# Issue order of the first decay loads, and longer rows in the w_in loads, in a fused state-space and feed-forward kernel

## The chip, the core and the metric

The kernel runs on one core of a Trainium2 chip. The time is device time in microseconds (us) of one execution; the median of the runs of the kernel before is 116.85 us. A core has a matrix engine (TensorE, PE in the profile; PEld is its weight load), VectorE (DVE), ScalarE (ACT), GpSimd (POOL) and SyncE (SP). Each works through its own instructions in order. DMAs are issued here by SP and ACT (SPq and ACTq in the profile) and carried by 16 DMA engines.

## The reference

A chunked state-space scan, followed by a feed-forward layer with a tanh-approximated GELU. In short, for x of shape (4, 8, 768, 32), decays a of shape (4, 8, 768), B and C of shape (4, 8, 768, 16):

```python
cum = np.cumsum(np.log(np.clip(a, 1e-6, 1)), axis=-1)      # within a chunk
M = (C @ B.T) * causal * np.exp(cum[i] - cum[j])
y = M @ x + (C @ state) * np.exp(cum)
state = np.exp(sum) * state + (B * decay_from_j).T @ x
# then, on y as (3072 tokens, 256):
h = y @ w_in                       # w_in: (256, 2048)
out = gelu_tanh(h) @ w_out         # w_out: (2048, 256)
```

All inputs and the output are fp32; the kernel multiplies in bf16.

## The kernel before

The scan works on chunks of Q = 128 positions, six to a batch entry, 24 in all; two chunks make a unit u (12 units). For each unit the kernel forms G = B C^T for all heads (f_G), masks it (f_M, on VectorE), transposes nothing more but multiplies by x and by the carried state (f_Y), and copies the result to SBUF as bf16 (f_yev, into xm). The decays are folded into B and C beforehand: the decay products are made by a scan (f_Rq), turned (f_tpq), inverted (f_recip0) and multiplied into C (f_mulc) and B (f_mulb). Each unit then goes through the feed-forward layer: eight pieces of the first matrix (f_s1, line 709), eight GELUs on ScalarE (f_gelu, line 713), and eight pieces of the second (f_s2, line 727) whose sum is copied out (f_oev) and stored.

The order of all this is written out by hand in the string ORDERED: each word is a step, a letter behind the colon is the engine (A = ScalarE, D = VectorE, P = GpSimd, S = SP), and ~n emits n filler matmuls of 128 columns on a zero matrix (function fill, line 697), grouped into matmuls of up to 512 columns. A step's instructions are emitted at its place, and every engine executes its own in that order. So a step that waits holds all later steps of its engine.

At the start, four loads (load_aq.0 to load_aq.3, line 159) fill aq_t, the decays of the first four chunks, one 32-row part each; f_clipq on VectorE needs all four. load_bc0.1 and load_bc0.0 (line 150) load C and B of the first four chunks, load_x4 (line 183) x of the same chunks, load_a.0 and load_a.1 (line 162) the remaining decays. Then come the weights: load_wi.0 to load_wi.3 (line 190) bring w_in in four blocks of 512 columns, both halves k of its 256 rows in one load; load_wo.0 to load_wo.3 (line 194) bring w_out in four blocks. A weight block lands as fp32 in a tile wf; two casts turn it into bf16: wi.q.k casts columns q*512 to (q+1)*512 of half k, wo.q.k half of a block of w_out. In the order string wi.0.0, wi.0.1, wi.1.0 and wi.3.0 are on ScalarE, wi.1.1, wi.2.0, wi.2.1 and wi.3.1 on GpSimd, where wo.0.1 stands ahead of wi.2.1; wo.0.0 is on VectorE.

s1.u.i computes columns i*256 to (i+1)*256 of the hidden layer for unit u, four matmuls; so s1.0.0 and s1.0.1 need wi.0.0 and wi.0.1, s1.0.2 and s1.0.3 need wi.1.0 and wi.1.1, s1.0.4 and s1.0.5 need wi.2.0 and wi.2.1.

Other steps that are spoken of: peq and ppq (the decay of a whole chunk, spread by a matmul at line 356 and copied by pendq); tw.i (transposes of C and B for the first four chunks, line 425) and ew (their copies out of PSUM); XX (matmuls that bring x of the first four chunks into row order, line 563) and xn.c (their copies, on ScalarE); XD.u (products of B and x, line 573), which are written into the same PSUM tiles that xn reads; S.u.k and SP.c (state updates on VectorE, lines 676 and 683); pp and pend (decays of all chunks, lines 393 and 314); mul1, T1, tp2 (the decayed B and C of chunks 4 and 5).

Of the kernel before, what the change touches and what calls it, by code (L numbers as in the profile page):

```python
# [8 lines left out]
FP32 = mybir.dt.float32  # L9
# [7 lines left out]

SCR = (2, 3)
ORDERED = """
c_wz c_ident c_zero c_unp load_aq.2:A load_bc0.1 c_tri load_aq.1:S load_aq.3:S load_aq.0:A c_m8  # L20
c_sel c_warm c_m4 load_bc0.0 load_x4 clipq Rq tpq load_a.0:A load_a.1:S peq ~53 ppq pendq:A
load_wi.0 c_cz c_bmask recip0 mulc.0:D mulc.1:D mulb:P ~9 tw.1 tw.0 ew.0.0:D c_par ew.0.1:A tw.2
ew.0.2:A x4.1:D ~8 G.0 clip ew.1.0:A ew.1.1:A load_wi.1 M.0.0 GE.3 x4.0:P GE.2 load_wi.2 ~2 XX.0
# [64 lines left out]
def kernel(  # L88
# [10 lines left out]
    nc = tc.nc  # L99

    batch, H, S, D = x.shape
# [20 lines left out]
    wfp = ctx.enter_context(tc.tile_pool(name="wfp", bufs=WFB))  # L122
# [22 lines left out]
    XF, X16, WF = {}, {}, {}  # L145
# [39 lines left out]
    wi = moe_w_in.rearrange("(k d) f -> d k f", d=128)  # L185
    wo = moe_w_out.rearrange("(q p k) m -> q p k m", p=128, k=4)

    def load_wi(q):
        WF[("i", q)] = wfp.tile([128, 2, 512], FP32, name="wf")
        nc.sync.dma_start(out=WF[("i", q)], in_=wi[:, :, q * 512:(q + 1) * 512])  # L190

    def load_wo(q):
        WF[("o", q)] = wfp.tile([128, 4, d_model], FP32, name="wf")
# [100 lines left out]
    w_in_sb = const.tile([128, 2, d_ff], BF16, name="w_in_sb")  # L294
# [17 lines left out]
    def copy(eng, o, i):  # L312
        if eng == "ACT":
            nc.scalar.activation(o, i, AF.Copy)  # L314
        elif eng == "POOL":
            nc.gpsimd.tensor_copy(out=o, in_=i)  # L316
        else:
            nc.vector.tensor_copy(out=o, in_=i)  # L318

    def f_wi(q, k, eng):  # L320
        copy(eng, w_in_sb[:, k, q * 512:(q + 1) * 512], WF[("i", q)][:, k])

    def f_wo(q, k, eng):
        copy(eng, w_out_sb[:, 4 * q + 2 * k:4 * q + 2 * k + 2], WF[("o", q)][:, 2 * k:2 * k + 2])
# [418 lines left out]
    def add(eng, fn, *args, deps=(), alt=""):  # L743
        name = ".".join([fn.__name__.removeprefix("f_"), *map(str, args)])
        s = steps[name] = Step(name, eng, None, deps, alt or eng)
        if alt:
            s.fn = lambda: fn(*args, {"A": "ACT", "D": "DVE", "P": "POOL", "S": "SP"}[s.eng])
        elif fn is f_s1:
            s.fn = lambda: fn(*args, s.pre)
        else:  # L750
            s.fn = lambda: fn(*args)
        return s
# [6 lines left out]
    bl = {(b, i): add("S", load_bc, b, i) for b in range(1, batch) for i in (1, 0)}  # L759
    xl = {u: add("S", load_x, u) for u in range(2, NU)}  # L760
    wl = {(k, q): add("S", f, q) for k, f in (("i", load_wi), ("o", load_wo)) for q in range(4)}

    win = {(q, k): add("P", f_wi, q, k, alt="PAD", deps=[wl[("i", q)]]) for q in range(4) for k in range(2)}
    won = {(q, k): add("P", f_wo, q, k, alt="PAD", deps=[wl[("o", q)]]) for q in range(4) for k in range(2)}
    for q in range(4):
        wl[("i", q)].takes("wf", win[(q, 0)], win[(q, 1)])
        wl[("o", q)].takes("wf", won[(q, 0)], won[(q, 1)])

    ccz, cid, ctri, cbm, cm8 = (add("P", f) for f in (c_cz, c_ident, c_tri, c_bmask, c_m8))
# [130 lines left out]
    for u in range(NU):  # L900
        for i in range(NI):
            q = (2 * i + 1) // 4
# [21 lines left out]
    for w in ORDERED.split():  # L924
        if w[0] == "~":
            fill(yb, int(w[1:]))
        else:
            w, _, n = w.partition("+")
            name, _, e = w.partition(":")
# [33 lines left out]
```

## Time and profile before

| | |
|---|---|
| runs of the kernel | 116.79 and 116.91 us, median 116.85 |
| span of the profiled execution, first to last instruction | 115.1 us |
| what the median has around that span | 1.75 us |
| TensorE busy | 109.4 us (95%) |
| ScalarE, VectorE, GpSimd busy | 75.1, 68.7, 15.1 us |
| DMA | 15.97 MB, mean 139 GB/s; issues of SP from 0.80 us on |

The profile is of one execution. Its own time outside the span is not recorded; the difference of 1.75 us stands in the table as the difference of the median and the span.

How to read the lines: the time line gives start, duration, engine, line of the kernel, operation, out<-in and the shapes, xN for N instructions merged, and in brackets the idle time of the engine before them with what ended it. The view by windows gives for a stretch its length, then the busy time of each engine in it with the number of instructions, then the granted TensorE clock, the mean busy share of the DMA engines and GB/s. DMA landings give the size and the time from issue to landing in us. The chain of work that ended last gives start, duration and what ran.

### The profile page before, as it was taken

What the parts mean: (1) busy time and instruction counts of PE and PEld (TensorE: products, weight loads), DVE (VectorE), ACT (ScalarE), POOL (GpSimd) and SP (SyncE); (2) the same over time, 40 slices, a digit from 0 to 9 for tenths busy, and PEclk for the clock granted to TensorE, in tenths of its full rate; (3) what the DMA queues carried; (4) which work ended last, traced back from release to release, by engine and by line L of the source; (5) the groups of instructions that cost most, each with busy time, mean ns of one, the idle gap of its engine ahead of it and who ended that gap; (6) DMA issues with size and microseconds to landing.
All of it is one profiled execution on the core that took longest, in us unless ns stands there. A gap on an engine that the chain in (4) does not pass through costs nothing.

```text
span 115.1 us, 3372 instructions
## 1 busy us (share of the span) xinstructions
PE 109.4 (95%) x1425; PEld 92.2 (80%) x1425; DVE 68.7 (60%) x135; ACT 75.1 (65%) x149; POOL 15.1 (13%) x32
## 2 busy tenths in 40 slices
PE   6999799999999999999999999999999999999990
PEld 2354578978877979799898998998989989999970
DVE  6688799998799989196966281546827421000100
ACT  3119889978657767657576486377766765685710
POOL 6564274122220000020002000000000000000000
PEclk9999999999999999999999999999999999999999
DMA  2999999949969828959478760000014014001132
GB/s 65 236 280 286 397 293 311 278 84 218 225 109 226 214 64 203 192 147 265 102 158 184 174 178 0 6 0 0 0 50 138 0 49 139 0 0 51 46 103 79
DMA packets 43006, 15.97 MB, mean 139 GB/s; under 512 B 36656, under 2 KB 41456, under 8 KB 42992
## 3 DMA queue, kind: packets, MB, share of 16 engines
q1 hardware_dynamic: 42848, 15.68, 53.9%
q8 instruction: 11, 0.18, 0.6%
q10 hardware_dynamic: 144, 0.08, 0.4%
q14 instruction: 3, 0.02, 0.1%
HBM read 11.04 MB, written 3.93 MB: 130 GB/s over the span
## 4 chain that ended last, share of the span: by engine, by line
PE 82%; DMA 8%; SPq 4%; POOL 1%; issue 1%; ACT 0%
PE hp L709 36%; PE o_ps L727 33%; DMA wf<-in_moe_w_out_dram 8%; PE yb L727 3%; PE ga L595 3%; PE yb L650 2%; PE yb L659 2%; SPq L190 1%; PE hp L628 1%; SPq L162 1%; SPq L159 1%; SPq L150 1%; POOL w_out_sb L316 1%; POOL w_in_sb L316 1%; SPq L183 1%
## 5 line engine op out<-in xcount | busy, mean ns | idle before, releaser
L713 ACT ACTIVATE gT<-hp 128x512 bf16<-128x512 f32 x96 | 53.3, 595 | 24.5 <-PE hp L709 24.0
L709 PE MATMUL hp<-xm,w_in_sb 128*128 128x256 bf16 x384 | 51.9, 273 | 0.5 <-ACT pend L314 0.3
L727 PE MATMUL o_ps<-w_out_sb,gT 128*128 128x256 bf16 x352 | 46.4, 273 | 0.0
L709 PEld LDWEIGHTS <-w_in_sb 128*128 128x128 bf16 x384 | 41.2, 114 | 3.2 <-issue 1.7
L727 PEld LDWEIGHTS <-gT 128*128 128x128 bf16 x384 | 37.0, 98 | 4.7 <-issue 0.8
L318 DVE COPY o_sb<-o_ps 128x256 f32<-128x256 f32 x7 | 3.0, 424 | 22.4 <-PE o_ps L727 18.4
L605 DVE TENSOR_TENSOR m<-ga,tri 128x1024 bf16<-128x1024 f32 x12 | 14.6, 1216 | 0.0
L605 DVE TENSOR_TENSOR m<-gb,tri 128x1024 bf16<-128x1024 f32 x11 | 13.4, 1219 | 0.5 <-PE gb L595 0.5
L697 PE MATMUL yb<-wz 128*128 128x512 bf16 (+2 forms) x24 | 8.2, 491 | 1.1 <-DVE warm L222 1.1
L314 ACT ACTIVATE o_sb<-o_ps 128x256 f32<-128x256 f32 x15 | 5.6, 382 | 4.1 <-PE o_ps L727 3.0
L683 DVE SCALAR_TENSOR_TENSOR sp_new<-s_new,pend,bmask 128x256 bf16<-128x256 f32 x17 | 8.0, 479 | 0.1
L316 POOL CAST x<-x_t 128x512 bf16<-128x512 f32 x5 | 3.2, 648 | 34.9 <-DMA x_t<-in_x_dram 22.9
L676 DVE SCALAR_TENSOR_TENSOR s_new<-s_new,pend,hp 128x64 f32<-128x64 f32 x13 | 3.6, 279 | 5.7 <-PE hp L628 5.5
L697 PEld LDWEIGHTS <-wz 128*128 128x128 bf16 x25 | 2.9, 126 | 5.0 <-issue 3.6
L659 PE MATMUL yb<-m,x 128*32 128x128 bf16 x192 | 6.1, 219 | 0.0
L650 PE MATMUL yb<-ce,sp_new 128*32 128x128 bf16 x160 | 5.3, 220 | 0.0
L595 PE MATMUL ga<-ce,bh 32*128 32x256 bf16 x48 | 4.7, 272 | 0.1
L314 ACT ACTIVATE xm<-yb 128x512 bf16<-128x512 f32 x8 | 4.8, 597 | 0.0
L595 PE MATMUL gb<-ce,bh 32*128 32x256 bf16 x48 | 4.7, 273 | 0.0
L727 PE MATMUL yb<-w_out_sb,gT 128*128 128x256 bf16 x32 | 4.1, 273 | 0.0
L659 PEld LDWEIGHTS <-x 128*32 128x32 bf16 x192 | 3.8, 97 | 0.4 <-issue 0.2
L650 PEld LDWEIGHTS <-sp_new 128*32 128x32 bf16 x160 | 3.0, 96 | 1.0 <-issue 1.0
(108 smaller groups left out, 78.4 us busy)
## 6 DMA issues: line engine op xcount, KB each, us to landing
out_dram<-o_sb SPq DMA_DIRECT2D x24, 128.0 KB, 2.0
x_t<-in_x_dram SPq DMA_DIRECT2D x20, 128.0 KB, 3.8
wf<-in_moe_w_in_dram SPq DMA_DIRECT2D x4, 512.0 KB, 8.3
wf<-in_moe_w_out_dram SPq DMA_DIRECT2D x4, 512.0 KB, 8.9
bc_t<-in_B_dram SPq DMA_DIRECT2D x3, 384.0 KB, 4.8
bc_t<-in_C_dram SPq DMA_DIRECT2D x3, 384.0 KB, 4.3
scr<-bc SPq DMA_DIRECT2D x4, 192.0 KB, 3.1
x_t<-in_x_dram SPq DMA_DIRECT2D x1, 512.0 KB, 4.8
```

The source lines that it names most:

```text
L314: nc.scalar.activation(o, i, AF.Copy)
L316: nc.gpsimd.tensor_copy(out=o, in_=i)
L595: nc.tensor.matmul(out=gbank(g)[:, 256 * k:256 * k + 256], lhsT=bh_of(2 * u + k)[gs], rhs=ce_of(2 * u + k)[gs], start=True, stop=True, til ...
L605: nc.vector.tensor_tensor(out=m_of(u)[:, 2 * i:2 * i + 2].rearrange("p g k e t -> p (g k e) t"), in0=gx[i].rearrange("p g (k t) -> p (g k) ...
L650: nc.tensor.matmul(out=y4[32 * j:32 * j + 32, k, w], lhsT=sp[:, 32 * h:32 * h + 32], rhs=ce_of(gc)[:, h % 2], start=first(j), stop=False, ...
L659: nc.tensor.matmul(out=y4[32 * j:32 * j + 32, k, w], lhsT=X16[u][:, k, 32 * h:32 * h + 32], rhs=m[:, h // 2, h % 2, :], start=first(j), st ...
L676: nc.vector.scalar_tensor_tensor(out=s_new, in0=state[("s", gc - 1)], scalar=pend_of(gc), in1=d, op0=ALU.mult, op1=ALU.add)
L683: nc.vector.scalar_tensor_tensor(out=sp_new.rearrange("p (g d) -> p g d", g=4), in0=(XN[0][:, H * D:H * D + 64] if gc == 0 else state[("s" ...
L697: nc.tensor.matmul(out=t[:, 0:m * 128], lhsT=wz, rhs=w3.to_broadcast([128, m, 128]), start=True, stop=True, skip_group_check=True)
L709: nc.tensor.matmul(out=hp[:, j * T:(j + 1) * T], lhsT=w_in_k[:, w, q, k], rhs=xm[:, w, u * T:(u + 1) * T], start=(w == 0), stop=(w == 1))
L713: nc.scalar.activation(gts[u][:, 2 * i:2 * i + 2], hps.pop((u, i)).rearrange("p (j t) -> p j t", j=2), AF.Gelu_apprx_tanh)
L727: nc.tensor.matmul(out=ops[gc], lhsT=gts[u][:, fi, k * Q:(k + 1) * Q], rhs=w_out_sb[:, fi, :], start=(fi == 0 and (u > 0 or k == 0)), stop ...
```

## The change

There are two parts. In the order string the four loads of aq_t stand together, with aq.2 and aq.0 on ACT's queue as before and aq.1 and aq.3 on SP's, and the load of C (load_bc0.1) comes behind them. And load_wi.0 to load_wi.3 are cut differently: a load brings 1024 columns of one half k instead of 512 columns of both; a row of it is 4096 bytes instead of 2048, and 128 rows instead of 256 make a load of the same 512 KB. Load 2h + k holds half k of columns h*1024 to (h+1)*1024. The casts keep their names, shapes, engines and order; cast wi.q.k reads load 2(q // 2) + k instead of load q. So wi.0.0 and wi.1.0 wait for load 0, wi.0.1 and wi.1.1 for load 1, wi.2.0 and wi.3.0 for load 2, wi.2.1 and wi.3.1 for load 3. The sequence of instructions on TensorE, VectorE, ScalarE and GpSimd is the same; on SP the load of C moves behind the two decay loads. Line numbers move by one or two.

```diff
 ORDERED = """
-c_wz c_ident c_zero c_unp load_aq.2:A load_bc0.1 c_tri load_aq.1:S load_aq.3:S load_aq.0:A c_m8
+c_wz c_ident c_zero c_unp load_aq.2:A load_aq.1:S load_aq.0:A load_aq.3:S load_bc0.1 c_tri c_m8
...
     def load_wi(q):
-        WF[("i", q)] = wfp.tile([128, 2, 512], FP32, name="wf")
-        nc.sync.dma_start(out=WF[("i", q)], in_=wi[:, :, q * 512:(q + 1) * 512])
+        h, k = divmod(q, 2)
+        WF[("i", q)] = wfp.tile([128, 1024], FP32, name="wf")
+        nc.sync.dma_start(out=WF[("i", q)], in_=wi[:, k, h * 1024:(h + 1) * 1024])
...
     def f_wi(q, k, eng):
-        copy(eng, w_in_sb[:, k, q * 512:(q + 1) * 512], WF[("i", q)][:, k])
+        h, r = divmod(q, 2)
+        copy(eng, w_in_sb[:, k, q * 512:(q + 1) * 512], WF[("i", 2 * h + k)][:, r * 512:(r + 1) * 512])
...
-    win = {(q, k): add("P", f_wi, q, k, alt="PAD", deps=[wl[("i", q)]]) for q in range(4) for k in range(2)}
+    win = {(q, k): add("P", f_wi, q, k, alt="PAD", deps=[wl[("i", 2 * (q // 2) + k)]]) for q in range(4) for k in range(2)}
...
-        wl[("i", q)].takes("wf", win[(q, 0)], win[(q, 1)])
+        wl[("i", q)].takes("wf", win[(q - q % 2, q % 2)], win[(q - q % 2 + 1, q % 2)])
```

## The prediction

> **What bounds the kernel now.** I read the page first, then the chain of work that ended last, then the time line of each engine up to 25 us, then the DMA landings.
>
> ```profile
> span 115.1 us, 3372 instructions
> PE 109.4 (95%) x1425; PEld 92.2 (80%) x1425; DVE 68.7 (60%) x135; ACT 75.1 (65%) x149; POOL 15.1 (13%) x32
> ```
> ```profile
> 17.60:112.00 94.40, 94.40 (x1243) 83.94 (x1243) 54.81 (x95) 64.49 (x125) 5.49 (x9) 1.00 0.50 118
> ```
> The second fence is the view by windows: from 17.6 us to the end TensorE is busy 94.40 of 94.40 us. So the kernel is a start of about 17.5 us and then a solid block of matmuls. The diff touches neither the number nor the order of the matmuls; whatever it gains or loses it does by moving the moment at which that block begins, and it can lose nothing later unless an operand comes late. The chain shows what sets that moment:
>
> ```profile
> 6.23 9.55 DMA wf<-in_moe_w_out_dram
> 15.83 0.87 POOL w_out_sb L316
> 16.70 0.76 POOL w_in_sb L316
> 17.51 0.96 PE hp L709 x7
> ```
> The weights arrive in one queue, behind each other; GpSimd casts them in order; the last of those casts (wi.2.1) releases the block at 17.51. Just ahead stands ScalarE, which casts the first weights, and all that is queued behind these casts:
>
> ```profile
> 11.19 0.39 ACT L314 ACTIVATE x<-hp 128x256 bf16<-128x256 f32 x1
> 11.78 1.15 ACT L314 ACTIVATE w_in_sb<-wf 128x512 bf16<-128x512 f32 x2 [0.19 <-DMA wf<-in_moe_w_in_dram]
> 12.83 0.37 ACT L314 ACTIVATE x<-hp 128x256 bf16<-128x256 f32 x1
> ...
> 13.16 0.61 POOL L316 CAST w_in_sb<-wf 128x512 bf16<-128x512 f32 x1 [1.72 <-DMA wf<-in_moe_w_in_dram]
> 13.25 0.18 PE L573 MATMUL hp<-x4b,bc0s 32*32 32x64 bf16 x1 [0.46 <-ACT x L314]
> ...
> 13.80 0.28 DVE L676 SCALAR_TENSOR_TENSOR s_new<-s_new,pendq,hp 128x64 f32<-128x64 f32 x1 [0.81 <-PE o_ps L573]
> ```
> The first w_in load lands just before 11.78 (ScalarE waited 0.19 us for it), the second just before 13.16 (GpSimd waited 1.72 us for it). Behind wi.0.0 and wi.0.1 on ScalarE comes xn.2 (12.83), which releases XD.1 on TensorE (13.25), which releases S.1.0 on VectorE (13.80).
>
> **Part 1: the decay loads go ahead of C.**
>
> ```profile
> 0.80 0.46 SPq L150 DMA_DIRECT2D bcf<-in_C_dram  x1
> ...
> 1.32 1.03 SPq L159 DMA_DIRECT2D aq_t<-in_a_dram  x2
> ...
> 2.39 0.42 SPq L150 DMA_DIRECT2D bcf<-in_B_dram  x1
> ...
> 4.10 0.17 DVE L277 TENSOR_REDUCE m<-ident 128x4 f32<-128x32 bf16 x1
> 5.16 0.23 DVE L328 TENSOR_SCALAR acq<-aq_t 128x128 f32<-128x128 f32 x1 [0.89 <-DMA aq_t<-in_a_dram]
> ...
> 6.37 1.05 POOL L416 TENSOR_TENSOR bc0s<-bcf,rt 128x512 bf16<-128x512 f32 x1 [1.74 <-DVE rt L342]
> ```
> ```profile
> aq_t<-in_a_dram ACTq DMA_DIRECT2D x1, 16.0 KB, 2.0
> bcf<-in_C_dram SPq DMA_DIRECT2D x1, 256.0 KB, 3.1
> bcf<-in_B_dram SPq DMA_DIRECT2D x1, 256.0 KB, 3.5
> ```
> The decay load that had the engines to itself landed 2.0 us after its issue; the last of the four, behind C, only at about 5.1, where VectorE's 0.89 us of idle time ends. With two issues of about 0.5 us on each queue from 0.80, all four land near 1.3 + 2.0 = 3.3. VectorE is busy until 4.10 + 0.17 = 4.27, so clipq moves from 5.16 to about 4.3: 0.86 us. No instruction is added; SP issues the same DMAs, C at 0.80 + 1.03 = 1.83 instead of 0.80, B and all behind it where they were. C lands at about 1.83 + 3.1 = 4.9, before its first reader (mulc, after recip0, near 5.9).
>
> How much of the 0.86 us gets through? Very little:
>
> ```profile
> 1.05 5.76 PE L697 MATMUL yb<-wz 128*128 128x512 bf16 x14 [1.05 <-DVE warm L222]
> ...
> 7.76 0.40 PE L425 MATMUL hp<-ident,cz 128*128 128x128 bf16 x4 [0.26 <-DVE cz L409]
> ```
> TensorE's order is fixed, and the filler matmuls ahead of ppq and tw.1 run until 7.50 (7.76 less 0.26 idle) whatever VectorE does. tw.1 can gain 0.26 us, not 0.86. mulb on GpSimd needs B besides: B landed at 2.39 + 3.5 = 5.9 and moves later (next paragraph), so mulb stays near its 6.37 and tw.0 near 8.0. I let 0.26 us through to ScalarE's xn.1, which then ends at 11.58 - 0.26 = 11.32, and there it meets the wait for the first weights at 11.78.
>
> What it costs: C's 256 KB start a microsecond later, and everything after C stands in the same queue.
>
> ```profile
> 2.00:4.00 2.00, 2.00 (x6) 0.62 (x5) 1.93 (x7) 1.23 (x2) 1.86 (x5) 1.00 0.90 191
> 4.00:6.00 2.00, 2.00 (x6) 0.73 (x5) 1.04 (x5) 0.00 (x0) 0.56 (x2) 1.00 1.09 274
> 6.00:7.00 1.00, 1.00 (x6) 0.52 (x5) 0.91 (x4) 0.00 (x0) 0.63 (x1) 1.00 1.16 288
> ...
> 7.75 0.76 POOL L316 CAST x4b<-x_t 128x512 bf16<-128x512 f32 x1 [0.33 <-DMA x_t<-in_x_dram]
> ```
> The last two columns are the DMA share and GB/s. The engines are nearly full from 2 us on, so a microsecond given away at the start cannot all be caught up: between 2 and 7 us stand 2 x 0.90 + 2 x 1.09 + 1.16 = 5.1 us of engine work, which at the 1.1 of the fuller windows takes 4.6 us; 0.4 us can be caught up, and the decay loads that run in the freed microsecond are a little more. Bounds: all caught up (0) and nothing caught up (1.0); I take 0.3, since x4 and B need less than the full share. x4 lands near 8.0 instead of 7.7. Its cast on GpSimd then ends at 8.8, and XX.0, which needs it, ran at 9.63: covered; the cover is gone at a shift of about 0.6.
>
> **Part 2: w_in in blocks of 4096-byte rows.** The same 512 KB a load, half as many rows; the casts keep their number and shape. Two things change.
>
> First, what a cast waits for. wi.0.0 (k = 0) needs load 0, wi.0.1 (k = 1) now needs load 1; before, both came out of load 0. On the time line the pair ends at 12.93 and its second cast, at the 0.61 us of a w_in cast, begins at 12.32; it would wait from there to the landing of load 1. Behind the waiting cast on ScalarE stand xn.2, yev.0, pend, wi.1.0 and the first gelu; TensorE (XD.1, then s1.0.0) and VectorE (S.1.0) wait for these. On GpSimd wi.2.1 now needs load 3 instead of load 2:
>
> ```profile
> 6.74 0.76 SPq L190 DMA_DIRECT2D wf<-in_moe_w_in_dram  x1
> ...
> wf<-in_moe_w_in_dram SPq DMA_DIRECT2D x1, 512.0 KB, 10.3
> ```
> Load 3 landed at 17.0, and moves to 17.3; wi.2.1 stood behind wo.0.1 until 16.65 anyway and now ends near 18.1 instead of 17.46: 0.6 us, less than what follows.
>
> Second, how fast the loads go. The views by windows:
>
> ```profile
> 9.00:10.00 1.00, 0.96 (x18) 0.57 (x17) 1.00 (x3) 1.00 (x4) 0.00 (x0) 1.00 0.87 240
> ...
> 12.00:13.00 1.00, 0.79 (x31) 0.49 (x26) 0.96 (x4) 1.00 (x3) 0.00 (x0) 1.00 1.04 416
> ...
> 19.00:20.00 1.00, 1.00 (x15) 0.99 (x12) 0.97 (x3) 1.00 (x3) 0.41 (x1) 1.00 1.01 373
> ```
> From 9 to 10 us only w_in rows of 2048 bytes move, at 240 GB/s. From 12 to 13 us w_in rows and the 4096-byte rows of w_out move together, at 416, and from 19 to 20 nearly nothing but w_out, at 373. So 2048-byte rows can go at full rate, and what slows the first two loads (5.4 us from x4's landing at 7.7 to load 1 at 13.1, where three later loads, to 17.0, took 3.9, or 1.3 each) is something the row's length does not obviously explain. Bounds for load 1: the slowness goes with the short rows and vanishes, 8.0 + 2 x 1.3 = 10.6; it stays and C's delay is added, 13.1 + 0.3 = 13.4 (14.1 with the whole microsecond). I take 13.4, by the nearest row: the same tensor at the same place in the stream.
>
> [...]
>
> The sum, on the profiled execution: wi.0.1 starts at 13.45 instead of 12.32, +1.13. xn.2, XD.1, S.1.0 and s1.0.0 follow by the same 1.1. TensorE had 0.25 us of slack before 17.51, where it waited for wi.2.1; VectorE had none after 13.80, and its results reach TensorE with a tenth to spare:
>
> ```profile
> 17.51 0.96 PE L709 MATMUL hp<-xm,w_in_sb 128*128 128x256 bf16 x7 [0.25 <-POOL w_in_sb L316]
> ...
> 19.16 0.52 DVE L435 TENSOR_TENSOR bc0s<-bcf,rt 128x256 bf16<-128x256 f32 x1
> ...
> 19.75 0.21 PEld L443 LDWEIGHTS <-bc0s 128*128 128x128 bf16 x2
> ```
> mul1.0 ends at 19.68, T1.0 begins at 19.75. So nearly all of VectorE's 1.1 us arrives in the block. The gain of Part 1 is swallowed in the wait. Span 115.1 + 1.1 = 116.2; the median of the two runs is 116.85, 1.75 above the span, which I add: **117.9 us**, 0.9% slower.
>
> **The rivals.** *The loads get faster, and it is not slower than before.* If the stalls belong to the 2048-byte rows, load 1 lands at 10.6 and the casts follow xn.1 at once: 11.32 instead of 11.78, and up to 0.6 if part 1 brings more than 0.26. Then XD.1 and S.1.0 come 0.5 to 0.6 earlier: 116.3. For it: 373 GB/s with long rows. Against it: 416 with short ones in the mix, so the length alone is not it. The point of decision is load 1 landing at 12.3; there the whole change is nothing (116.9), which is the case of half the stalls gone.
>
> *The clock.*
>
> ```profile
> 10.40 0.88 PE L697 MATMUL yb<-wz 128*128 128x512 bf16 x4
> ...
> 12.51 0.29 PE L659 MATMUL yb<-m,x 128*32 128x128 bf16 x8
> ```
> The fillers up to 6.8 us took 5.76 us for 14 matmuls, 0.41 each; the later ones, at 10.40, take 0.88 for four, 0.22 each. If TensorE, which would stand almost idle from the end of Y.0 at 12.8 to XD.1 at 14.4 (1.6 us), falls back to that pace, it runs at half speed for up to the same 5.5 us and loses up to 2.8: 120.7. Against it: the windows show a granted clock of 1.00 through all the gaps up to 0.46 us, and no gap as long as this one, so nothing here shows the threshold. [...]
>
> *The queue loses more.* C's whole microsecond, and stalls a third longer: load 1 at 15, +2.7, 119.5.
>
> **How the numbers follow.** The wait on load 1 as forecast (117.4 to 118.5): 0.50. Loads faster, 116.0 to 116.6: 0.30. Half of it, about 116.9: 0.10. Clock or a slower queue, over 119: 0.10. The range that leaves out less than 2 in 10: 116.1 to 118.7; the likeliest case's own is 117.4 to 118.5. A measurement of this kernel can tell about 2% from no change, 2.3 us: faster by more would need the block to start at 15.2, which no case gives, 0.03; slower by more is the last case and a little beyond, 0.11; within, 0.86.
>
> **What would show it.** clipq near 4.3 and no wait there; tw.1 still at about 7.5; C landing near 4.9 and x4 near 8.0; ScalarE with a wait of about a microsecond for w_in between the two casts of wi.0; XD.1 at about 14.4 and S.1.0 at 14.9; the GB/s of the windows in which only w_in moves still near 250. The prediction is wrong if these windows show 370 or more, or if load 1 lands before 12.3.

## The result, and the profile after

The changed kernel takes 119.86 us, median of two runs (119.75 and 119.97); before, it was 116.85. The ratio is 1.0252, with a 95% interval of 1.022 to 1.0285: slower by 3.0 us, where 1.1 was forecast. The ratios with intervals in this document leave out executions more than 1.5% above the fastest of their kernel; the medians given beside them are of all executions, which are counted by their granted clock, as that turns out to be the matter here.

The span is 118.3 us, 3.2 more than before. From the page of the kernel after, the span, the busy times, and the granted clock in 40 slices of 2.96 us:

```profile
span 118.3 us, 3372 instructions
PE 110.6 (94%) x1425; PEld 93.2 (79%) x1425; DVE 67.8 (57%) x135; ACT 75.4 (64%) x149; POOL 16.0 (14%) x32
...
PEclk9999855999999999999999999999999999999999
```

The same instructions, and nearly the same busy times; but in slices 5 to 7 the clock is below 9, where the page of before has a 9 everywhere. Next the windows of after. The columns after the length are PE, PEld, DVE, ACT and POOL busy, then clock, DMA share and GB/s:

```profile
8.00:9.00 1.00, 0.96 (x16) 0.42 (x12) 0.91 (x4) 0.68 (x3) 0.61 (x1) 1.00 1.02 299
9.00:10.00 1.00, 1.00 (x49) 0.56 (x41) 1.00 (x3) 1.00 (x3) 0.10 (x1) 1.00 0.91 258
10.00:11.00 1.00, 0.96 (x36) 0.43 (x13) 0.78 (x2) 0.99 (x4) 1.00 (x2) 1.00 0.95 299
12.50:14.40 1.90, 0.00 (x0) 0.00 (x0) 0.17 (x1) 1.14 (x4) 0.61 (x1) 0.88 1.03 410
14.00:17.00 3.00, 2.24 (x41) 1.77 (x41) 1.94 (x5) 1.85 (x6) 1.39 (x3) 0.50 1.09 327
17.00:20.00 3.00, 3.00 (x15) 1.94 (x14) 2.89 (x9) 2.08 (x5) 2.01 (x3) 0.50 0.92 277
21.00:115.00 94.00, 94.00 (x1242) 83.71 (x1240) 52.28 (x87) 64.15 (x124) 5.53 (x7) 1.00 0.47 107
```

And the stretch around the gap of the kernel before:

```profile
12.50:14.40 1.90, 1.16 (x61) 1.03 (x48) 1.06 (x7) 1.66 (x5) 0.61 (x1) 1.00 1.04 393
14.00:17.00 3.00, 2.58 (x22) 2.24 (x21) 3.00 (x7) 2.70 (x7) 1.78 (x3) 1.00 1.10 306
17.00:20.00 3.00, 2.75 (x53) 2.18 (x51) 2.89 (x7) 2.85 (x6) 1.62 (x3) 1.00 0.94 302
```

From 12.5 to 14.4 us TensorE does nothing at all. From 14 to 20 us it runs at a clock of 0.50, where before had 1.00. From 21 us on the block is as solid as before. So the 3.2 us are made between 11 and 21 us. (The column of the clock says 1.00 ahead of the first rise too, though the first fillers ran at half pace: the record of the clock in a trace begins with that rise, here at 3.71 us, in the profile of before at 6.62.)

ScalarE's time line of after around the weight casts:

```profile
10.87 0.39 ACT L315 ACTIVATE x<-hp 128x256 bf16<-128x256 f32 x1
12.14 0.63 ACT L315 ACTIVATE w_in_sb<-wf 128x512 bf16<-128x512 f32 x1 [0.88 <-DMA wf<-in_moe_w_in_dram]
13.53 0.63 ACT L315 ACTIVATE w_in_sb<-wf 128x512 bf16<-128x512 f32 x1 [0.76 <-DMA wf<-in_moe_w_in_dram]
14.06 0.36 ACT L315 ACTIVATE x<-hp 128x256 bf16<-128x256 f32 x1
```

The two casts of wi.0, a pair of 1.15 us before, stand apart: the second waits 0.76 us for load 1, and behind it xn.2 starts at 14.06 instead of 12.83. What it releases, on TensorE and on VectorE:

```profile
14.48 0.21 PE L575 MATMUL hp<-x4b,bc0s 32*32 32x64 bf16 x1 [2.01 <-ACT x L315]
...
15.72 1.87 PE L711 MATMUL hp<-xm,w_in_sb 128*128 128x256 bf16 x8 [0.28 <-ACT pend L315]
17.42 0.59 PE L699 MATMUL hp<-wz 128*128 128x512 bf16 x1
17.81 1.91 PE L711 MATMUL hp<-xm,w_in_sb 128*128 128x256 bf16 x8
...
23.00 0.28 PE L445 MATMUL ga<-ident,bc0s 128*128 128x128 bf16 x2
```
```profile
15.06 0.28 DVE L678 SCALAR_TENSOR_TENSOR s_new<-s_new,pendq,hp 128x64 f32<-128x64 f32 x1 [2.40 <-PE o_ps L575]
```

The same steps on TensorE before:

```profile
14.18 1.03 PE L709 MATMUL hp<-xm,w_in_sb 128*128 128x256 bf16 x8 [0.28 <-ACT pend L314]
...
15.67 1.03 PE L709 MATMUL hp<-xm,w_in_sb 128*128 128x256 bf16 x8
...
19.85 0.28 PE L443 MATMUL ga<-ident,bc0s 128*128 128x128 bf16 x2
```

Taken apart at three marks, the loss adds up. XD.1 starts at 14.48 instead of 13.25: +1.23, the wait. s1.0.0 starts at 15.72 instead of 14.18: +1.54, so 0.31 more is lost between the two, where XD.1 and pp already run at half clock. T1 starts at 23.00 instead of 19.85: +3.15, so 1.61 more. From T1 to the last instruction both executions take the same, 95.2 to 95.3 us, so T1 holds the whole loss. By these marks the wait costs 1.23 us and what follows it 0.31 + 1.61 = 1.92; eight matmuls of s1 take 1.87 and 1.91 us where they took 1.03. This is a split by time and not yet by cause: the experiments show that a wait at XD.1 need not reach T1 in full.

Two other parts of the start. The first fillers of after, on TensorE, and the transposes behind them:

```profile
1.05 4.33 PE L699 MATMUL yb<-wz 128*128 128x512 bf16 x14 [1.05 <-DVE warm L223]
...
6.42 0.40 PE L427 MATMUL hp<-ident,cz 128*128 128x128 bf16 x4
7.66 0.40 PE L427 MATMUL o_ps<-ident,bc0s 128*128 128x128 bf16 x4 [0.85 <-POOL bc0s L418]
```

and the chain of work that ended last, its part before 14.2 us:

```profile
1.72 0.42 SPq L150
...
2.18 0.58 SPq L150
...
5.41 8.09 DMA wf<-in_moe_w_in_dram
...
13.53 0.63 ACT w_in_sb L315
```

C is issued at 1.72, B at 2.18, and load 1 lands at 5.41 + 8.09 = 13.50. The chain now runs through this landing and the second cast of wi.0, where before it ran through w_out and GpSimd.

### The profile page after: what moved, and what is told of

The parts are those of the page before. It is cut to its first block, busy times and chain, and to the rows that moved or that the text cites. A ratio compares the mean times of both kernels' runs of the same rounds, so it can differ in the third digit from the quotient of the medians.

```text
span 118.3 us, 3372 instructions
## 1 busy us (share of the span) xinstructions
PE 110.6 (94%) x1425; PEld 93.2 (79%) x1425; DVE 67.8 (57%) x135; ACT 75.4 (64%) x149; POOL 16.0 (14%) x32
## 4 chain that ended last, share of the span: by engine, by line
PE 85%; DMA 7%; SPq 4%; ACT 1%; issue 0%
PE hp L711 38%; PE o_ps L729 33%; DMA wf<-in_moe_w_in_dram 7%; PE yb L729 3%; PE ga L597 3%; PE yb L652 2%; PE yb L661 2%; SPq L162 1%; PE hp L630 1%; SPq L150 1%; SPq L159 1%; SPq L183 1%; ACT w_in_sb L315 1%; PE hp L395 0%; PE hp L699 0%
## 5 line engine op out<-in xcount | busy, mean ns | idle before, releaser
L711 PE MATMUL hp<-xm,w_in_sb 128*128 128x256 bf16 x384 | 53.7, 280 | 0.3 <-ACT pend L315 0.3
L729 PE MATMUL o_ps<-w_out_sb,gT 128*128 128x256 bf16 x352 | 46.9, 274 | 0.0
L711 PEld LDWEIGHTS <-w_in_sb 128*128 128x128 bf16 x384 | 42.0, 115 | 3.6 <-issue 1.6
L607 DVE TENSOR_TENSOR m<-gb,tri 128x1024 bf16<-128x1024 f32 x11 | 13.4, 1219 | 0.5 <-PE gb L597 0.3
L317 POOL CAST x<-x_t 128x512 bf16<-128x512 f32 x5 | 4.3, 861 | 37.1 <-ACT o_sb L315 19.0
L699 PE MATMUL yb<-wz 128*128 128x512 bf16 (+2 forms) x24 | 6.7, 420 | 1.1 <-DVE warm L223 1.1
```

The source lines that it names most:

```text
L607: nc.vector.tensor_tensor(out=m_of(u)[:, 2 * i:2 * i + 2].rearrange("p g k e t -> p (g k e) t"), in0=gx[i].rearrange("p g (k t) -> p (g k) ...
L699: nc.tensor.matmul(out=t[:, 0:m * 128], lhsT=wz, rhs=w3.to_broadcast([128, m, 128]), start=True, stop=True, skip_group_check=True)
L711: nc.tensor.matmul(out=hp[:, j * T:(j + 1) * T], lhsT=w_in_k[:, w, q, k], rhs=xm[:, w, u * T:(u + 1) * T], start=(w == 0), stop=(w == 1))
L729: nc.tensor.matmul(out=ops[gc], lhsT=gts[u][:, fi, k * Q:(k + 1) * Q], rhs=w_out_sb[:, fi, :], start=(fi == 0 and (u > 0 or k == 0)), stop ...
```

## The experiments

There were two theories. The first: the wait on load 1 accounts for everything, and the slow matmuls merely go along with it. The second: the gap that the wait opens lowers TensorE's clock, and that costs more than the wait. A third question was why the first w_in loads are slow. A granted clock of 1.000 over the span means full speed from the first rise on; 0.985 means one stretch of about 3.4 us at half (0.5 x 3.4 / 117 = 0.015; in the profile with short rows below, 15.4 to 18.8 us), which the expectations call a half window; 0.971 means two (in the profile above 6.8 us, from 13.95 to 20.77); means of 0.996 and above are counted as full (0.996 over a span of 114.7 us leaves 0.9 us at half). The two runs of the changed kernel above had 0.971. On the three chips of the experiments, the kernel before had one such stretch in 14 of 79 executions and never two.

### Each part alone

The decay loads first, w_in as before:

```diff
-c_wz c_ident c_zero c_unp load_aq.2:A load_bc0.1 c_tri load_aq.1:S load_aq.3:S load_aq.0:A c_m8
+c_wz c_ident c_zero c_unp load_aq.2:A load_aq.1:S load_aq.0:A load_aq.3:S load_bc0.1 c_tri c_m8
```

> The order of the decay loads alone, w_in in the blocks of before. Clock theory (the loss is the cast's wait on load 1, which empties TensorE for 2 us, and the half clock that follows): no cast waits for a second load, so TensorE's gap stays under 1 us, the granted clock stays 1.00, and the time is within 0.6 us of before, 116.6 to 117.4. Queue theory (the loss is C's microsecond, passed on to every load): most of the 3.0 us is here, 118.5 or more.

The w_in blocks and casts of the changed kernel, the order string of before:

```diff
-        WF[("i", q)] = wfp.tile([128, 2, 512], FP32, name="wf")
-        nc.sync.dma_start(out=WF[("i", q)], in_=wi[:, :, q * 512:(q + 1) * 512])
+        h, k = divmod(q, 2)
+        WF[("i", q)] = wfp.tile([128, 1024], FP32, name="wf")
+        nc.sync.dma_start(out=WF[("i", q)], in_=wi[:, k, h * 1024:(h + 1) * 1024])
```

> The w_in blocks alone, the decay loads in the order of before. Clock theory: load 1 lands near 13.1, the second cast waits for it, TensorE's gap is 1.3 to 1.7 us; if that is enough to halve the clock, 119.0 to 119.6, if not, 117.5 to 117.9. Queue theory: C starts in time, nothing is late, 116.6 to 117.2.

Part 1 alone: median 117.36 of ten against 117.29 of before on that chip, ratio 0.9999 (0.9951 to 1.0046). No gain, as forecast; but the clock did not stay at 1.00 throughout, as was expected: four of the ten had one stretch at half (117.65 to 118.85), where before had five of 25. Part 2 alone: median 118.46; three executions at full clock (116.78 to 117.06), six with one stretch at half (118.13 to 118.98), one with two (120.68). Its ratio, 1.0014 (0.9959 to 1.007), rests on the five shortest, three of them at full clock. So most of the loss comes with part 2, and in steps that go with the clock: the medians of the three groups are 116.92, 118.77 and 120.68. In its profiled execution the wait was there, and small:

```profile
11.70 0.64 ACT L315 ACTIVATE w_in_sb<-wf 128x512 bf16<-128x512 f32 x1
12.83 0.63 ACT L315 ACTIVATE w_in_sb<-wf 128x512 bf16<-128x512 f32 x1 [0.49 <-DMA wf<-in_moe_w_in_dram]
```

### The gap filled

The changed kernel with 32 filler matmuls more ahead of Y.0, on an engine that only waits there:

```diff
-load_bc1.0 xn.2:A ME.3:P ME.2:P pe Y.0 XD.1 pp yev.0.0.2:A S.1.0 load_wo.1 load_bc1.1 SP.1 S.1.1
+load_bc1.0 xn.2:A ME.3:P ME.2:P pe ~32 Y.0 XD.1 pp yev.0.0.2:A S.1.0 load_wo.1 load_bc1.1 SP.1 S.1.1
```

> The changed kernel with 32 blocks of filler matmuls (1.7 us) ahead of Y.0, in the time in which TensorE stood empty; nothing else is changed. Clock theory: the granted clock stays 1.00 to the end and the time falls by about 1.8 us to 117.9 to 118.3, although work was added. Wait theory (all 3.0 us come from the late casts and what stands behind them): no change, 119.7 to 120.1.

All ten executions ran at full clock: median 117.69, ratio to before 1.0049 (1.0019 to 1.0079). That is a little below the expected 117.9 to 118.3. More work, and 2.2 us less than the two runs of the changed kernel above, 0.7 less than its median on two other chips (118.43 and 118.44, below). The load was nearly as late as above, on ScalarE:

```profile
11.74 0.63 ACT L315 ACTIVATE w_in_sb<-wf 128x512 bf16<-128x512 f32 x1 [0.49 <-DMA wf<-in_moe_w_in_dram]
13.16 0.63 ACT L315 ACTIVATE w_in_sb<-wf 128x512 bf16<-128x512 f32 x1 [0.80 <-DMA wf<-in_moe_w_in_dram]
```

and the windows show what is different:

```profile
12.50:14.40 1.90, 1.90 (x63) 0.92 (x60) 0.15 (x1) 0.97 (x3) 0.61 (x1) 1.00 1.02 406
14.00:17.00 3.00, 2.47 (x69) 2.03 (x56) 2.23 (x5) 2.56 (x7) 1.23 (x2) 1.00 1.10 325
17.00:20.00 3.00, 3.00 (x56) 2.57 (x54) 2.89 (x8) 2.86 (x7) 2.09 (x3) 1.00 0.96 306
```

TensorE is busy 1.90 of 1.90 us in the old gap, and the clock stays at 1.00. The wait is kept, the gap is filled, and 0.5% remains. This is the test that decides between the two theories: the first would have kept the loss or added to it.

The trace also shows what the wait cost at full clock in this execution. XD.1 started at 14.21, 0.96 us later than before, and T1 at 20.41, only 0.56 later:

```profile
14.21 0.20 PE L575 MATMUL hp<-x4b,bc0s 32*32 32x64 bf16 x1
...
20.41 0.27 PE L445 MATMUL ga<-ident,bc0s 128*128 128x128 bf16 x2
```

### Short rows, the same waits

The changed kernel, its loads of 1024 columns cut into rows of 2048 bytes (the tile is padded between the two):

```diff
-        WF[("i", q)] = wfp.tile([128, 1024], FP32, name="wf")
-        nc.sync.dma_start(out=WF[("i", q)], in_=wi[:, k, h * 1024:(h + 1) * 1024])
+        WF[("i", q)] = wfp.tile([128, 2, 516], FP32, name="wf")
+        nc.sync.dma_start(out=WF[("i", q)][:, :, 0:512],
+                          in_=wi[:, k, h * 1024:(h + 1) * 1024].rearrange("d (r f) -> d r f", r=2))
```

> The changed kernel with the same blocks, but each row of 4096 bytes brought as two of 2048 bytes (the tile is padded between them). If the row's length is worth nothing, the second w_in load lands at 13.4 to 13.7 and the time is that of the changed kernel, 119.6 to 120.2. If the long rows save time on the queue, it lands later by 0.3 us or more and the time is 120.3 or more.

Median 118.73 of four (three with one stretch at half clock, one with two), ratio 1.0141 (1.0067 to 1.0215). Load 1 was no later for the short rows:

```profile
13.25 0.63 ACT L316 ACTIVATE w_in_sb<-wf 128x512 bf16<-128x512 f32 x1 [0.82 <-DMA wf<-in_moe_w_in_dram]
```

The windows from 8, 9 and 10 us moved 338, 283 and 301 GB/s, against 299, 258 and 299 of the long rows. In these two executions the longer rows bring nothing; it is one trace each, and the landing of load 1 varies more than that between executions of one kernel (below). The time was expected at 119.6 or more, by the two runs above; it came lower, with one stretch in three of the four.

By chance this trace prices one stretch. XD.1 started at 14.20, as with the gap filled (14.21), but from 15.4 to 18.8 us the clock was at half (0.50), and T1 came 1.21 us later than there:

```profile
21.62 0.28 PE L446 MATMUL ga<-ident,bc0s 128*128 128x128 bf16 x2
```

### The changed kernel again, on two other chips

No edit; a fresh sample of the kernel that was run twice above.

> The changed kernel itself, more executions. Clock theory: the granted clock of the execution (the share of full speed) decides. [...] Wait theory: every execution is at 119.7 to 120.1, whatever the clock.

> The changed kernel once more, beside the kernel before on this chip. Clock theory: three groups by granted clock, 117.0 to 118.0 at 1.00, 118.2 to 118.9 at 0.985, 119.7 or more at 0.971, with at least six in ten below 1.00; the median is 0.6 to 1.5 us above the kernel before on the same chip. If the first two executions (119.75 and 119.97) are its usual time, the median is 119.5 or more.

On the first of these chips: median 118.43 of ten against 117.57 of before; three at full clock, seven with one stretch at half. On the second: 118.44 of twelve against 117.14; three full (116.26 to 117.56), five with one (118.12 to 119.19), four with two (119.99 to 120.56). With the two runs above that makes 24 executions: 6 full, 116.26 to 118.00; 12 with one, 118.1 to 119.2; 6 with two, 119.75 to 120.56. The first two both belong to the last group. At full clock the medians are 117.36 of three against 117.47 of before's eighteen there, and 117.17 of three against 117.06 of 27: no difference that so few can show. The ratios, 1.0042 (0.999 to 1.0094) and 0.9985 (0.9924 to 1.0045), show none either, but four of the seven executions behind the first have a stretch at half clock. By medians of all executions the change costs 0.9 and 1.3 us, not 3.0, and what it does is to make half clock the rule.

The landing of load 1 varies too. The profiled execution on the first of the two chips, ScalarE, then TensorE's waits (engine, line, what for: total, times, longest):

```profile
11.92 0.63 ACT L315 ACTIVATE w_in_sb<-wf 128x512 bf16<-128x512 f32 x1 [0.16 <-DMA wf<-in_moe_w_in_dram]
```
```profile
PE hp L711 <- POOL w_in_sb L317: 1.2, 1, 1.2
...
PE hp L575 <- ACT x L315: 0.4, 1, 0.4
```

Load 1 let its cast start at 11.92, not 13.53, from the same code; XD.1 waited 0.4 us, and the clock stayed full. But it gained nothing: s1 then waited 1.2 us for wi.2.1, which now needs load 3 and started at 17.36. T1 came at 20.38, 0.53 later than before, and the span was 115.6. The execution on the second chip waited in the old place, and its clock fell in slices 5 and 6:

```profile
PE hp L575 <- ACT x L315: 1.6, 1, 1.6
```
```profile
PEclk9999967999999999999999999999999999999999
```

### The casts behind what TensorE waits for

The changed kernel, the two casts of wi.0 moved behind xn.2 and yev.0 on ScalarE:

```diff
-XD.0 load_wo.0 xn.0:A ew.1.2:A SP.0 S.0.0 xn.1:A wi.0.0:A wi.0.1:A R ~13 G.1 S.0.1 load_wi.3 XX.1
-load_bc1.0 xn.2:A ME.3:P ME.2:P pe Y.0 XD.1 pp yev.0.0.2:A S.1.0 load_wo.1 load_bc1.1 SP.1 S.1.1
+XD.0 load_wo.0 xn.0:A ew.1.2:A SP.0 S.0.0 xn.1:A R ~13 G.1 S.0.1 load_wi.3 XX.1
+load_bc1.0 xn.2:A ME.3:P ME.2:P pe Y.0 XD.1 pp yev.0.0.2:A wi.0.0:A wi.0.1:A S.1.0 load_wo.1 load_bc1.1 SP.1 S.1.1
```

> The changed kernel with wi.0.0 and wi.0.1 moved behind xn.2 and yev.0 on ScalarE; loads, blocks and engines as in the change. If the path goes through what is queued behind the waiting cast (xn.2, XD.1, S.1.0), S.1.0 starts near 13.2 instead of 15.06 and, where the clock stays full, the time is 116.7 to 117.3. If load 1 itself is the bound (s1.0.0 cannot begin before its cast), s1.0.0 starts at 14.4 or later and the time at full clock is 117.4 or more. Half windows should be fewer than in the changed kernel, since the gap is shorter.

VectorE's first state update of unit 1, and the casts on ScalarE:

```profile
13.09 0.28 DVE L678 SCALAR_TENSOR_TENSOR s_new<-s_new,pendq,hp 128x64 f32<-128x64 f32 x1 [0.29 <-PE o_ps L575]
```
```profile
13.15 1.14 ACT L315 ACTIVATE w_in_sb<-wf 128x512 bf16<-128x512 f32 x2
```

S.1.0 starts at 13.09 instead of 15.06, and the casts, now later in the queue, find their loads landed. Median 117.36 of ten, six at full clock, four with one stretch; ratio 0.9979 (0.9936 to 1.0021), where the changed kernel on the same chip had a median of 118.43. Load 1 was late in this execution too: GpSimd's wi.1.1, which needs it as well, waited for it until 13.60.

```profile
13.60 0.63 POOL L317 CAST w_in_sb<-wf 128x512 bf16<-128x512 f32 x1 [2.35 <-DMA wf<-in_moe_w_in_dram]
```

So S.1.0 was early because it no longer stood behind the cast, and the 1.07 us by which the median is lower were lost in the steps queued behind it. Four stretches in ten against seven in ten is too few to show by itself that the clock falls less often. It is level with before, not faster: TensorE waited 0.6 us for wi.2.1 instead, and T1 came at 20.45.

### Before, without its fillers

Can gaps lower the clock in the kernel before too, with no load late?

```diff
-ew.0.2:A x4.1:D ~8 G.0 clip ew.1.0:A ew.1.1:A load_wi.1 M.0.0 GE.3 x4.0:P GE.2 load_wi.2 ~2 XX.0
-XD.0 load_wo.0 xn.0:A ew.1.2:A SP.0 S.0.0 xn.1:A wi.0.0:A wi.0.1:A R ~13 G.1 S.0.1 load_wi.3 XX.1
+ew.0.2:A x4.1:D G.0 clip ew.1.0:A ew.1.1:A load_wi.1 M.0.0 GE.3 x4.0:P GE.2 load_wi.2 XX.0
+XD.0 load_wo.0 xn.0:A ew.1.2:A SP.0 S.0.0 xn.1:A wi.0.0:A wi.0.1:A R G.1 S.0.1 load_wi.3 XX.1
```

> The kernel before without the fillers of 8, 2 and 13 blocks ahead of G.0, XX.0 and G.1; no load, cast or product is changed. Clock theory: TensorE's busy share of the windows around 10 us falls by a third, half windows appear in more executions than in the kernel before (5 of 25 at 0.985), and those take 1.5 to 2 us more than the others, though no load is late. Queue and wait theories: same as before, 116.5 to 117.3, with no more half windows than before.

All ten executions fell to half clock, eight of them for two stretches and two for one: median 118.59 against 117.57, ratio 1.0089 (1.0025 to 1.0153), for seven matmuls less (23 x 128 columns). The longest waits of TensorE after its start, and the window ahead of the fall, which came at 13.05:

```profile
PE ga L595 <- ACT ce L314: 1.4, 2, 0.9
```
```profile
9.60:13.10 3.50, 2.50 (x84) 1.65 (x81) 3.14 (x8) 3.50 (x10) 1.22 (x2) 0.99 0.97 330
13.10:19.80 6.70, 6.30 (x59) 4.45 (x59) 5.58 (x13) 4.44 (x10) 3.45 (x5) 0.50 0.94 286
```

No gap is longer than 0.9 us, and yet the clock falls to 0.50: here it did not take one long gap. TensorE was busy for 2.50 of the 3.50 us ahead of it.

### Could part 1 be made to pay?

In the profile of part 1 alone tw.0 waited 0.85 us for mulb, which needs B, so B was put ahead of C, on the old w_in blocks; once with four executions, then with twelve on another chip, and there also with eight fillers ahead of Y.0:

```diff
-c_sel c_warm c_m4 load_bc0.0 load_x4 clipq Rq tpq load_a.0:A load_a.1:S peq ~53 ppq pendq:A
+c_sel c_warm c_m4 load_bc0.1 load_x4 clipq Rq tpq load_a.0:A load_a.1:S peq ~53 ppq pendq:A
```

> The order of part 1 alone, with the old w_in blocks, and B loaded ahead of C. In part 1 alone tw.0 waited 0.85 us for mulb, which waits for B. If B's landing is the bound there, mulb starts about 1 us earlier, tw.0 runs right behind tw.1 near 6.9 and the time at full clock falls by 0.3 to 0.5 us, to 116.2 to 116.6. If C, now landing near 6.2, takes B's place as the bound, tw.1 waits instead and the time is that of part 1 alone, 116.4 to 117.1.

> The decay loads first, B ahead of C, the old w_in blocks, with more executions, since four were too few. Clock theory: executions at full clock take 116.0 to 116.8, about 1 us less than the kernel before at full clock; one in four has a half window and takes 117.9 to 118.3; faster than before by 0.5 to 1%. If the four were luck, the two medians at full clock lie within 0.3 us.

> The same with 8 blocks of filler matmuls (0.43 us) ahead of Y.0, which stands on the path. Clock theory: fewer half windows than without the fillers, at most one in ten, and 0.2 to 0.5 us more at full clock, 116.4 to 117.0. If half windows are not a matter of TensorE's share of busy time, they are as many as without, and the whole kernel is slower by the fillers.

The four looked like a gain, 0.9895 (0.978 to 1.0011); the twelve did not bear it out: 1.0034 (1.0001 to 1.0067), median 117.82 against 117.14, five of them with a stretch at half clock. With the fillers: median 116.97, ten of twelve at full clock, one with one stretch and one with two, ratio 0.997 (0.9938 to 1.0002). The median is 0.85 us lower with the fillers, in the same direction as above, though ten full-clock executions of twelve against seven is too little to show it by itself. No version tried is clearly faster than before.

### A w_out block ahead of w_in

Are the loads slow because they are w_in, or because they come first?

```diff
-load_wi.0 c_cz c_bmask recip0 mulc.0:D mulc.1:D mulb:P ~9 tw.1 tw.0 ew.0.0:D c_par ew.0.1:A tw.2
+load_wo.0 load_wi.0 c_cz c_bmask recip0 mulc.0:D mulc.1:D mulb:P ~9 tw.1 tw.0 ew.0.0:D c_par ew.0.1:A tw.2
```

(with load_wo.0 taken out at its old place)

> The kernel before with the first block of w_out (contiguous, rows of 4096 bytes) loaded ahead of the first block of w_in; one look, for the rate of the first weight load. If the slow start belongs to w_in's rows, the windows from 7.5 to 9 us now run at 370 GB/s or more and the w_in block behind it is slow. If it belongs to the place in the stream, w_out's block is slow there, 240 to 300 GB/s. The first GELU comes about a microsecond later, so the time itself is 117.5 to 119.5 either way.

One execution, 117.19 us beside 117.47 of before, below the expected 117.5 to 119.5. Three windows of it:

```profile
8.00:9.00 1.00, 0.82 (x13) 0.79 (x14) 0.62 (x3) 0.38 (x1) 0.83 (x1) 1.00 0.98 365
9.00:10.00 1.00, 0.96 (x12) 0.30 (x9) 1.00 (x6) 0.94 (x4) 0.00 (x0) 1.00 1.05 358
10.00:11.00 1.00, 1.00 (x42) 0.61 (x42) 1.00 (x1) 1.00 (x2) 0.36 (x1) 1.00 0.98 322
```

With w_out first and w_in behind it, 365, 358 and 322 GB/s were moved, where before had 240 from 9 to 10 us and the changed kernel 258. By this execution neither the place in the stream nor w_in alone would explain the slow start. But load 1 of the changed kernel released its cast at 13.53, 13.10 and 11.92 in three executions, so one execution settles nothing here, and the cause stays open.

## Why the prediction was wrong

Step by step, by the prediction's own terms:

- *clipq near 4.3, with no wait*: right; it started at 4.20. The decay loads landed 1.9 us (ACT's queue) and 1.7 us (SP's) after their issue.
- *tw.1 held by the fillers until 7.50*: wrong for this execution, without consequence. The clock rose to full earlier, the first fillers took 4.33 us instead of 5.76, and tw.1 started at 6.42. The next to come late was what the prediction named, mulb with B: tw.0 waited 0.85 us for it and started at 7.66. xn.1 ended at 11.26; 11.32 was forecast.
- *The queue loses 0.3 us*: somewhat more. C landed 3.5 us after 1.72, at 5.2 (4.9 forecast), and GpSimd's cast of x4, waiting for its data, started at 8.24 (landing forecast near 8.0).
- *Load 1 at 13.4, wi.0.1 starts at 13.45*: 13.50 and 13.53. *XD.1 14.4, S.1.0 14.9*: 14.48 and 15.06. The largest term of the sum, +1.13, measured 1.23 at XD.1.
- *Nearly all of VectorE's 1.1 us arrives in the block*: too much. With the gap filled and the clock full, 0.96 us at XD.1 arrived at T1 as 0.56.
- *w_in alone still moves near 250 GB/s, and the row's length brings nothing*: 258 to 299, and the one trace with short rows shows no difference.
- *Load 3 at 17.3, and wi.2.1 behind it less than what follows*: its cast started at 17.42 after a wait of 0.73 us. In this execution TensorE did not wait for it; in the two traces of the new blocks in which XD.1 was early (12.88 and 12.54) it was the wait that came last, and T1 was late by 0.53 and 0.60 us all the same.
- *The clock stays at 1.00 through the gap*: this is the step that failed. The prediction saw it as a rival, in a case that shared a chance of 0.10 with a slower queue; the runs show it as the rule for this kernel, 18 of 24 executions. It had the gap at 1.6 us (2.01 measured) and its price at up to 2.8 us (1.92 by the marks above; one stretch measured 1.21 by the pair of traces with XD.1 at 14.20 and 14.21).

Two numbers that come near are luck. The rival of a slower queue had 119.5, close to 119.86, but by a load 1 at 15 us, which landed at 13.50. And the medians on the two other chips, 118.43 and 118.44, lie in the range of the prediction's likeliest case, but most of those executions had the half clock that this case leaves out, and the wait alone costs less than it says.

What misled was how the gaps of before were read. The trace of before had no gap over 0.46 us, so it could not exclude a fall. The prediction says so itself, and still gave the clock only a part of 0.10. No run shows a length of gap that is safe: without the fillers the clock fell with none over 0.9 us. And the prediction asked about the length of one gap, where that run lost the clock with several short ones. TensorE's busy time over a few microseconds does not tell the cases apart either. A stretch with a busy share of 0.71 kept the clock, and one with 0.72 lost it (all are as long as one stretch at half clock, 3.41 us, half of the 6.83 in the profile after):

| stretch, us | TensorE busy | clock behind it |
|---|---|---|
| changed kernel, first profile, 10.53 to 13.95 | 1.86 of 3.42 (0.54) | half for 6.8 us |
| changed kernel, last chip, 12.10 to 15.51 | 1.53 of 3.41 (0.45) | half for 3.4 us |
| before without fillers, 9.63 to 13.04 | 2.47 of 3.41 (0.72) | half for 6.8 us |
| changed kernel, first profile, 5.35 to 8.76 | 2.26 of 3.41 (0.66) | full, to 13.95 |
| before, 12.25 to 15.66 | 2.42 of 3.41 (0.71) | full |

What sets the clock is therefore not shown. What the runs show is how often it fell: in all ten executions without the fillers, in none of ten with the gap filled, in 18 of 24 of the changed kernel and in 14 of 79 of the kernel before.

The stretches at half clock last 3.4 or 6.8 us, and the times at full clock between two changes came out as whole multiples of 3.41 us too: 10.24 and 99.0 us in the profile after, 109.2 in that of before. The first rise comes at 3.71 us in the profile after and at 6.62 in that of before, though both kernels begin with the same fillers. That one kernel's executions had no stretch, one or two came with no change of its code, and the runs do not show what decides among them.

The other way in which the prediction could have gone wrong was real as well: load 1 landed early in one profiled execution. It brought nothing, as wi.2.1 then came last. The prediction's main case (the wait, at full clock) is seen best with the gap filled: 117.69, 0.4 us above the median of before on that chip, where 1.1 was forecast.

## What to carry to other kernels

When a change adds a wait on the way to TensorE, price not only the wait but the clock behind it. Here the clock fell behind one gap of 2.01 us, and in the kernel without fillers behind several of at most 0.9 us. So where a change opens such gaps, put one or two stretches of half speed into the sum (3.4 us each here, and one cost 1.21 us). Fillers in such a gap cost little, as the engine is waiting anyway, and here 1.9 us of them kept the clock in ten executions of ten. And ask of every wait what stands behind it in its engine's queue: moving two waiting casts behind the steps that TensorE needs brought the median back to that of before.

## What the runs showed that was not expected

- The clock fell after a window in which TensorE was busy for 72% of the time (without fillers, 2.47 of 3.41 us from 9.63), with no gap over 0.9 us, and once at half it stayed there through a window busy for 76% (changed kernel, 2.60 of 3.41 us from 13.95) and one busy for 87% (without fillers, 2.96 of 3.41 from 13.05).
- One kernel's executions fall into groups by the number of half-clock stretches: 116.3 to 118.0, 118.1 to 119.2 and 119.8 to 120.6 us for the changed kernel. Two runs can both lie in one group, as the first two did; four executions of the version with B ahead of C showed a gain that twelve did not.
- The same load in the same place of the same kernel released its cast at 11.92, 13.10 and 13.53 us in three executions.
